# Two head pairs to one probabilities-times-V run in a fused attention, MLP and expert kernel, with four resident weight blocks in place of five

## The chip, the cores and the metric

The kernel runs on one core of a Trainium2 chip. The metric is the device time of one execution in microseconds (us), as the median over runs. Five engines work side by side, each through its own list of instructions in order: TensorE (PE, with its weight loads shown apart as PEld), VectorE (DVE), ScalarE (ACT), GpSimd (POOL) and SyncE (SP, which here issues only DMA transfers). An instruction that waits holds up everything behind it on its engine.

## The reference

```python
def reference(q, k, v, w_in, w_out, w_gate, w_noise, noise, w1, w2):   # q, k, v: 4 x 8 x 576 x 64
    scores = q @ k^T / sqrt(64)
    keep the 32 largest scores of every row, softmax over them
    x = (attn @ v) as 2304 tokens x 512
    h = x @ w_in                                  # 512 x 2048
    x = (h * clip(h + 3, 0, 6) / 6) @ w_out       # 2048 x 512
    noisy = x @ w_gate + log1p(exp(x @ w_noise)) * noise      # 8 experts
    top-2 experts of each token, softmax over the two
    out[token] += weight * (relu(x @ w1[e]) @ w2[e])          # w1: 8 x 512 x 1024
```

## The kernel before, in words

Matrix products that need full precision are done with every operand split into a high and a low part, as three matmuls (high by high, high by low, low by high).

**Layer one** (`phase_a`) is a software pipeline, one step for each of 144 slots. A slot is one tile of 128 tokens (18 tiles) with one head (8 heads). Every stage of a slot stands at a fixed number of steps behind its start: the scores (`s`, PE) and their copy to SBUF (`ss`, ACT) first, then the search for the 32nd largest score (`seg`, `a`, DVE), the exponentials (`e`) and the mask (`z`, `y`, `t`), the transposition of the probabilities on PE (`pa`, evacuated by ACT into `pt` and `ph`), and the product with V (`av`). The heads are taken in pairs from there on. In the kernel before `av(p)` runs in every second step: 20 matmuls with the V of two heads as weights (16 with `pt`, 4 with `ph`), then one transposition that spreads the reciprocal row sums (`rb`, made by POOL from `sum`) over partitions. Two steps later ACT copies both halves to `xs` (128x256), POOL multiplies the product with the reciprocals (128x128), and another two steps later ACT and POOL make the high and low part of `xT`.

In the same steps runs the MLP of the chunk of two tiles before: 16 blocks of 128 hidden columns a chunk, `h` (12 matmuls, `mm1`), the gate (`r`, `g`; on ACT, DVE and POOL) and `xa` (6 matmuls, `mm2`). In some steps more stands: the transposition of a head's K (`kp`), and the router of finished tiles (`lt`, `lg`, `po`, and the scatters `idw` on POOL that tell which token goes to which expert).

A block of split MLP weights is 1 MB. Some blocks are resident in the ring "wr" (`NRES` buffers); the others are written to DRAM once (`wscr`) and fetched by SP for every chunk into the ring "ws" (`NSTR`, 4 buffers), three steps ahead in the program. After the last tile the chunk's blocks run without attention beside them.

**Layer two** (`phase_b`) is nine jobs (an expert's gathered tokens) of eight blocks each: `hb` (`mm1`), `hh` (ACT and DVE), `ac` (`mm2`). Weights of block g+3 are loaded into "ws" as `r2_` by SP and split into "wr" as `w2_` by ACT and DVE, or by ACT and POOL from the third job on. The tokens of a job come by `id` (SP, reads what the `idw` scatters wrote), `xg` (POOL, indirect gather) and `et` (PE transposition). Jobs after the first two add to rows already in the output: `old` (POOL gather) and a scatter at a job's end.

The order on PE, DVE, ACT and POOL is the program's from step 22 of layer one on; before that step and in layer two a list scheduler sets it. The order of SP's transfers is the scheduler's everywhere. What the change touches are these lines of the step and of the set of streamed blocks:

```python
stream = set(fb for fb in range(NFB) if (fb * (NFB - NRES)) // NFB != ((fb + 1) * (NFB - NRES)) // NFB)
if ok(x1) and x1 % 2 == 0: xscale(x1 // 2)        # ACT, before the search
if ok(x1) and x1 % 2 == 0: xscale2(x1 // 2)       # POOL, behind it
if ok(av_) and av_ % 2: av(av_ // 2)              # PE, behind mm2
if ok(x2) and x2 % 2 == 0: xsplit(x2 // 2)        # ACT and POOL
```

Of the kernel before, what the change touches and what calls it, by code (L numbers as in the profile page):

```python
# [7 lines left out]
F32 = mybir.dt.float32  # L8
# [5 lines left out]
ALU = mybir.AluOpType  # L14
# [13 lines left out]
NRES = 5  # L28
# [13 lines left out]
PTB = 3  # L42
# [4 lines left out]
VB = 10  # L47
# [7 lines left out]
XSB = 2  # L55
# [121 lines left out]
def phase_a(tc, pools, ident, q, k, v, w_in, w_out, X, worst, wscr, stream, begin, on_chunk=None, slots=NSLOT, pace=None):  # L177
# [46 lines left out]
    def copy(kind, out, in_):  # L224
        (nc.vector.tensor_copy if kind in ONV else nc.scalar.copy)(out, in_)
# [226 lines left out]
    def av(p):  # L452

        t = p // 4
        AVP[p] = o = ps.tile([128, 512], F32, name=f"av{p}", tag="av")
        for b, row, n, s0 in pieces(t):
            for j in range(5):
                for hh in (1, 0):
                    half = slice(64 * hh, 64 * hh + 64)
                    vt, pt = V[b, (2 * p + hh) % 8][:, j, :], PT[2 * p + hh][:, j, :] if j < 4 else PH[p]  # L460
                    nc.tensor.matmul(o[half, row:row + n], vt, pt[:, row:row + n], start=(j == 0),
                                     stop=(j == 4), skip_group_check=True)
        nc.tensor.transpose(o[:, 128:256], RB.pop(p).rearrange("p a b -> p (a b)"), ident)

    def xscale(p):
        xs = ap.tile([128, 256], F32, name=f"xs{p}", tag="xs", bufs=XSB)
        copy('a', xs, AVP.pop(p)[:, 0:256])
        XR[p] = xs

    def xscale2(p):  # L470
        xs = XR.pop(p)
        nc.gpsimd.tensor_tensor(xs[:, 0:128], xs[:, 0:128], xs[:, 128:256], op=ALU.mult)
        XS[p] = xs[:, 0:128]

    def xsplit(p):
        t, d = divmod(p, 4)
        c, j = chunk_of[t]
        if j == 0 and d == 0:
            xt = mp.tile([128, 2, 4, 256], F32R, name=f"xT{c}", tag="xT", bufs=2)
            XT[c] = [xt[:, z] for z in range(2)]  # L480
        xt, xs = XT[c], XS.pop(p)
        sl = slice(j * 128, (j + 1) * 128)
        copy('x', xt[0][:, d, sl], xs)
        nc.gpsimd.tensor_tensor(xt[1][:, d, sl], xs, xt[0].bitcast(F32)[:, d, sl], op=ALU.subtract)
# [99 lines left out]
    for st in range(-6, end):  # L584
# [33 lines left out]
        if ok(x1) and x1 % 2 == 0: xscale(x1 // 2)  # L618
# [19 lines left out]
        if ok(x1) and x1 % 2 == 0: xscale2(x1 // 2)  # L638
# [6 lines left out]
        if ok(av_) and av_ % 2: av(av_ // 2)  # L645
        for i, (dl, b, h) in enumerate(ksched):
            if dl + VL == st: v_load(i)
        if ok(x2) and x2 % 2 == 0: xsplit(x2 // 2)
# [678 lines left out]
```

## Time and profile before

| | |
|---|---|
| median of 3 runs | 1391.53 us (1387.91 to 1395.7) |
| the profiled execution | 1381.3 us; its span from first to last instruction 1379.5 us |
| mean granted TensorE clock | 0.975 |
| busy share of PE, DVE, ACT, POOL | 94%, 69%, 56%, 60% |
| streamed MLP blocks | 99 reads of 1 MB into "ws", 11 writes of 1 MB to `wscr` |

The profiled execution is 10.2 us shorter than the median of the runs. Layer one fills the first 880 us or so, layer two the rest. A busy PE is not a PE at its peak, so the page's shares say which engine is loaded, and the rows of a stretch say what it waits for there.

### The profile page before, as it was taken

What the parts mean: (1) busy time and instruction counts of PE and PEld (TensorE: products, weight loads), DVE (VectorE), ACT (ScalarE), POOL (GpSimd) and SP (SyncE); (2) the same over time, 40 slices, a digit from 0 to 9 for tenths busy, and PEclk for the clock granted to TensorE, in tenths of its full rate; (3) what the DMA queues carried; (4) which work ended last, traced back from release to release, by engine and by line L of the source; (5) the groups of instructions that cost most, each with busy time, mean ns of one, the idle gap of its engine ahead of it and who ended that gap; (6) DMA issues with size and microseconds to landing.
All of it is one profiled execution on the core that took longest, in us unless ns stands there. A gap on an engine that the chain in (4) does not pass through costs nothing. (4 is left out here: it accounts for less than half of the span.)

```text
span 1379.5 us, 27084 instructions
## 1 busy us (share of the span) xinstructions
PE 1293.2 (94%) x9006; PEld 1121.2 (81%) x9006; DVE 948.3 (69%) x3560; ACT 770.2 (56%) x1709; POOL 829.9 (60%) x1159
## 2 busy tenths in 40 slices
PE   5878899999999989999999899899999999999996
PEld 3554689989888878898988688788988898898985
DVE  7999987899987978869989753446353545435241
ACT  6888777777778666777777554534322322222220
POOL 7666777677767786767687845133324547465451
PEclk9789999999999999999999999999999999999999
DMA  7776644545365353445544447846446556465431
GB/s 249 261 279 226 230 145 157 193 166 176 132 206 166 127 149 124 170 131 187 175 143 157 123 154 246 265 140 221 136 153 195 178 167 204 140 214 177 137 109 38
DMA packets 138100, 239.56 MB, mean 174 GB/s; under 512 B 39779, under 2 KB 93155, under 8 KB 123872
## 3 DMA queue, kind: packets, MB, share of 16 engines
q1 hardware_dynamic: 127600, 210.57, 46.1%
q0 software_dynamic: 10352, 27.18, 5.9%
q8 instruction: 73, 1.20, 0.4%
q14 instruction: 75, 0.61, 0.2%
HBM read 209.08 MB, written 31.64 MB: 174 GB/s over the span
## 5 line engine op out<-in xcount | busy, mean ns | idle before, releaser
L959 PE MATMUL ac<-w,hh 128*128 128x512 f32 x960 | 247.8, 400 | 1.6 <-ACT hh L941 1.5
L935 PE MATMUL hb<-xe,w 128*128 128x320 f32 (+2 forms) x1536 | 239.4, 311 | 1.0 <-DVE hh L942 0.5
L935 PEld LDWEIGHTS hb<-xe,w 128*128 128x128 f32 x1536 | 232.1, 189 | 10.0 <-issue 3.9
L87 DVE MAX8 seg<-ss 128x8 f32<-128x82 f32 (+1 forms) x1008 | 213.9, 231 | 4.1 <-ACT ss L87 3.7
L87 POOL TENSOR_TENSOR y<-z,ss 128x576 f32<-128x576 bf16 x144 | 205.3, 1426 | 11.7 <-DVE z L87 10.1
L941 ACT ACTIVATE hh<-hb 128x640 fp32r<-128x640 f32 (+2 forms) x72 | 46.6, 647 | 295.7 <-PE hb L935 295.7
L959 PEld LDWEIGHTS ac<-w,hh 128*128 128x128 f32 x960 | 172.8, 188 | 40.3 <-ACT hh L941 5.4
L942 DVE SCALAR_TENSOR_TENSOR hh<-hb,hh 128x640 fp32r<-128x640 f32 (+2 forms) x72 | 53.9, 749 | 213.2 <-ACT hh L941 213.2
L87 PE MATMUL h<-xT,ws 128*128 128x256 f32 x1188 | 159.1, 283 | 9.3 <-DVE r L87 7.9
L87 ACT COPY ss<-s 128x576 f32<-128x576 f32 x144 | 92.6, 643 | 134.6 <-DVE e L87 69.6
L87 PE MATMUL xa<-ws,g 128*128 128x512 f32 x594 | 163.9, 410 | 2.2 <-POOL g L87 0.9
L87 PEld LDWEIGHTS h<-xT,ws 128*128 128x128 f32 x1188 | 150.0, 190 | 12.8 <-DVE r L87 9.9
L921 POOL TENSOR_TENSOR w<-r,w 128x1024 fp32r<-128x1024 f32 x40 | 97.9, 2452 | 85.2 <-ACT w L919 73.4
L87 DVE SCALAR_TENSOR_TENSOR e<-ss,t,e 128x576 f32<-128x576 f32 x144 | 147.6, 1025 | 0.1
L87 POOL TENSOR_TENSOR g<-r,g 128x256 fp32r<-128x256 f32 x124 | 100.2, 808 | 39.8 <-issue 19.6
L87 PEld LDWEIGHTS xa<-ws,g 128*128 128x128 f32 x594 | 104.0, 190 | 23.6 <-POOL g L87 5.1
L87 DVE TENSOR_SCALAR_CACHE_REDUCE z<-ss,a 128x576 bf16<-128x576 f32 x144 | 115.8, 804 | 0.2
L87 ACT ACTIVATE e<-ss,a 128x576 f32<-128x576 f32 x144 | 110.6, 768 | 1.4 <-POOL a L87 1.4
L87 PE MATMUL s<-kt,qt 128*128 128x288 f32 x512 | 101.2, 321 | 7.8 <-ACT qt L87 6.8
L87 DVE MAX8 t<-y 128x8 f32<-128x584 f32 x144 | 107.8, 749 | 0.0
L975 POOL DMA_INDIRECT out_dram<-y,id x40 | 41.8, 1045 | 108.9 <-DVE y L974 86.7
L87 PE MATMUL pa<-ident,e 128*128 128x128 f32 x576 | 91.3, 283 | 15.4 <-DVE e L87 13.4
(427 smaller groups left out, 2617.2 us busy)
## 6 DMA issues: line engine op xcount, KB each, us to landing
ws<-wscr SPq DMA_DIRECT2D x99, 1024.0 KB, 4.8
r<-in_moe_w_dram SPq DMA_DIRECT2D x144, 256.0 KB, 3.1
wscr<-wsp SPq DMA_DIRECT2D x11, 1024.0 KB, 5.8
wraw<-in_moe_w_in_dram SPq DMA_DIRECT2D x16, 512.0 KB, 4.2
wraw<-in_moe_w_out_dram SPq DMA_DIRECT2D x16, 512.0 KB, 5.1
ck<-in_moe_w_in_dram SPq DMA_DIRECT2D x32, 256.0 KB, 3.4
ck<-in_moe_w_out_dram SPq DMA_DIRECT2D x32, 256.0 KB, 3.2
out_dram<-zero SPq DMA_DIRECT2D x18, 256.0 KB, 4.2
```

The costliest lines, as they stand in the source:

```text
L87: o = f(*args, **kw)
L921: eng.tensor_tensor(w[:, 1], r, w.bitcast(F32)[:, 0], op=ALU.subtract)
L935: o = nc.tensor.matmul(p[:, half, 0:hn], w[:, a, d, :], XE[job][:, b, d, half * hn:(half + 1) * hn], start=(m == 0), stop=(m == 11))
L941: nc.scalar.activation(hv[:, 0], p[:, 0:nh, 0:hn], AF.Relu)
L942: LOW[:] = [STT(hv[:, 1], p[:, 0:nh, 0:hn], 0.0, h.bitcast(F32)[:, :, 0:n].rearrange("p a (b n) -> p a b n", b=nh)[:, 0], op0=ALU.max, op1 ...
L959: o = nc.tensor.matmul(ACC[job, j], h[:, a, j * 128:(j + 1) * 128], w[:, b, :], start=(x % NF2 == 0 and m == 0), stop=(x % NF2 == NF2 - 1 ...
L975: s = nc.gpsimd.indirect_dma_start(out=out, out_offset=bass.IndirectOffsetOnAxis(ap=t.bitcast(I32)[:, j, 1:2], axis=0), in_=y, in_offset=N ...
```

## The change

Two head pairs are taken together. `av(g)` runs in every fourth step: 20 matmuls for pair 2g, 20 for pair 2g+1, then both transpositions of `rb`, all into one PSUM bank. ACT's copy to `xs` becomes one of 128x512 in every fourth step, POOL's product one of 128x256, and the cast and the subtraction into `xT` one of 128x256 each. The probabilities of the first pair are held longer, so the ring of `pt` grows from 3 to 5 buffers and that of V from 10 to 12, while `xs` has 1 buffer instead of 2. For the space `NRES` goes from 5 to 4: blocks 0, 4, 8 and 12 stay resident in place of 0, 3, 6, 9 and 12, and 12 of 16 blocks stream instead of 11 (108 reads and 12 writes of 1 MB). The ring "wr" of 4 also holds the split weights of layer two.

```diff
-NRES = 5
+NRES = 4
-PTB = 3
+PTB = 5
-VB = 10
+VB = 12
-XSB = 2
+XSB = 1
-    def av(p):
-        t = p // 4
-        AVP[p] = o = ps.tile([128, 512], F32, name=f"av{p}", tag="av")
-        for b, row, n, s0 in pieces(t):
-            for j in range(5):
-                for hh in (1, 0):
-                    half = slice(64 * hh, 64 * hh + 64)
-                    vt, pt = V[b, (2 * p + hh) % 8][:, j, :], PT[2 * p + hh][:, j, :] if j < 4 else PH[p]
-                    nc.tensor.matmul(o[half, row:row + n], vt, pt[:, row:row + n], start=(j == 0),
-                                     stop=(j == 4), skip_group_check=True)
-        nc.tensor.transpose(o[:, 128:256], RB.pop(p).rearrange("p a b -> p (a b)"), ident)
+    def av(g):
+        t = g // 2
+        AVP[g] = o = ps.tile([128, 4, 128], F32, name=f"av{g}", tag="av")
+        for z in range(2):
+            p = 2 * g + z
+            for b, row, n, s0 in pieces(t):
+                for j in range(5):
+                    for hh in (1, 0):
+                        half = slice(64 * hh, 64 * hh + 64)
+                        vt, pt = V[b, (2 * p + hh) % 8][:, j, :], PT[2 * p + hh][:, j, :] if j < 4 else PH[p]
+                        nc.tensor.matmul(o[half, z, row:row + n], vt, pt[:, row:row + n], start=(j == 0),
+                                         stop=(j == 4), skip_group_check=True)
+        for z in range(2):
+            nc.tensor.transpose(o[:, 2 + z], RB.pop(2 * g + z).rearrange("p a b -> p (a b)"), ident)
...
-        copy('a', xs, AVP.pop(p)[:, 0:256])
+        copy('a', xs, AVP.pop(g))
...
-        nc.gpsimd.tensor_tensor(xs[:, 0:128], xs[:, 0:128], xs[:, 128:256], op=ALU.mult)
+        nc.gpsimd.tensor_tensor(xs[:, 0:2], xs[:, 0:2], xs[:, 2:4], op=ALU.mult)
...
-        copy('x', xt[0][:, d, sl], xs)
-        nc.gpsimd.tensor_tensor(xt[1][:, d, sl], xs, xt[0].bitcast(F32)[:, d, sl], op=ALU.subtract)
+        copy('x', xt[0][:, d:d + 2, sl], xs)
+        nc.gpsimd.tensor_tensor(xt[1][:, d:d + 2, sl], xs, xt[0].bitcast(F32)[:, d:d + 2, sl], op=ALU.subtract)
...
-        if ok(x1) and x1 % 2 == 0: xscale(x1 // 2)
+        if ok(x1) and x1 % 4 == 2: xscale(x1 // 4)
...
-        if ok(x1) and x1 % 2 == 0: xscale2(x1 // 2)
+        if ok(x1) and x1 % 4 == 2: xscale2(x1 // 4)
...
-        if ok(av_) and av_ % 2: av(av_ // 2)
+        if ok(av_) and av_ % 4 == 3: av(av_ // 4)
...
-        if ok(x2) and x2 % 2 == 0: xsplit(x2 // 2)
+        if ok(x2) and x2 % 4 == 2: xsplit(x2 // 4)
```

Three places show how instructions move. The first is SP at the end of layer one: `ws8_13` to `ws8_15` are the last three streamed MLP blocks of the last chunk, `id0` is the list of tokens of layer two's first job, `r2_0` and `r2_1` are raw weights of its first blocks. Before:

```order
L496 DMA ws8_13_13601<-wscr_78 128x2048
L496 DMA ws8_14_13628<-wscr_78 128x2048
L888 DMA id0_13871<-idw_76 128x6
L496 DMA ws8_15_13655<-wscr_78 128x2048
L911 DMA r2_0_13883<-in_moe2_w1_dram 128x4x128
L913 DMA r2_0_13883<-in_moe2_w2_dram 128x512
L911 DMA r2_1_13889<-in_moe2_w1_dram 128x4x128
```

and with the change:

```order
L499 DMA ws8_13_13404<-wscr_78 128x2048
L891 DMA id0_13674<-idw_76 128x6
L499 DMA ws8_14_13431<-wscr_78 128x2048
L499 DMA ws8_15_13458<-wscr_78 128x2048
L914 DMA r2_0_13686<-in_moe2_w1_dram 128x4x128
L916 DMA r2_0_13686<-in_moe2_w2_dram 128x512
L914 DMA r2_1_13692<-in_moe2_w1_dram 128x4x128
L916 DMA r2_1_13692<-in_moe2_w2_dram 128x512
```

`id0`, which reads what the `idw` scatters wrote, now stands ahead of the last two blocks instead of the last one.

The second is PE at the hand-over from layer one to layer two: `lt17`, `lg16` and `lg17` are router matmuls of the last two tiles, `po16` is the count that the router's placing of these tiles needs, `hb` and `ac` are layer two's first and second product. Before:

```order
L718 MATMUL lt17_13790<-ident_66,xm17_13769 128x128 x4
L729 MATMUL lg16_13784<-wgn_957,lx16_13782 128x16 x4
L729 MATMUL lg17_13797<-wgn_957,lx17_13795 128x16 x4
L935 MATMUL hb0_13922<-xe0_13882,w2_0_13886 128x384 x12
L959 MATMUL ac0_0_13974<-w2_0_13886,hh0_13935 128x512 x2
L959 MATMUL ac0_1_13978<-w2_0_13886,hh0_13935 128x512 x2
L959 MATMUL ac0_2_13982<-w2_0_13886,hh0_13935 128x512 x2
L935 MATMUL hb1_13958<-xe0_13882,w2_1_13892 128x384 x12
L959 MATMUL ac0_0_13974<-w2_0_13886,hh0_13935 128x512
L959 MATMUL ac0_1_13978<-w2_0_13886,hh0_13935 128x512
L959 MATMUL ac0_2_13982<-w2_0_13886,hh0_13935 128x512
L784 LDWEIGHTS tri_969
```

There `po16` stands behind `hb1` and three `ac`. With the change the order begins so:

```order
L721 MATMUL lt17_13593<-ident_66,xm17_13572 128x128 x4
L938 MATMUL hb0_13725<-xe0_13685,w2_0_13689 128x384 x12
L732 MATMUL lg16_13587<-wgn_939,lx16_13585 128x16 x4
L732 MATMUL lg17_13600<-wgn_939,lx17_13598 128x16 x4
L962 MATMUL ac0_1_13781<-w2_0_13689,hh0_13738 128x512 x2
L962 MATMUL ac0_2_13785<-w2_0_13689,hh0_13738 128x512 x2
L938 MATMUL hb1_13761<-xe0_13685,w2_1_13695 128x384 x12
```

and `po16` follows some blocks later:

```order
L938 MATMUL hb2_13795<-xe0_13685,w2_2_13701 128x384 x12
L962 MATMUL ac0_0_13777<-w2_1_13695,hh1_13774 128x512
L962 MATMUL ac0_1_13781<-w2_1_13695,hh1_13774 128x512
L962 MATMUL ac0_2_13785<-w2_1_13695,hh1_13774 128x512
L962 MATMUL ac0_0_13777<-w2_2_13701,hh2_13808 128x512 x2
L962 MATMUL ac0_1_13781<-w2_2_13701,hh2_13808 128x512 x2
L962 MATMUL ac0_2_13785<-w2_2_13701,hh2_13808 128x512 x2
L787 LDWEIGHTS tri_951
L787 MATMUL po16_13640<-oh16_13577,tri_951 128x16
```

`hb0` has moved ahead of `lg16` and `lg17`, and `po16` has moved behind `hb2` and the `ac` around it, directly ahead of `hb3`.

The third is POOL at a boundary of layer two's jobs, where `old` and `xg0` are gathers and `w2_36` to `w2_38` the low parts of split weights. Before:

```order
L921 TENSOR_TENSOR w2_36_15693<-r2_36_15690,w2_36_15693 128x1024
L975 DMA out_0_dram<-y3_2_15583,id3_14559 2304x512
L975 DMA out_0_dram<-y3_3_15588,id3_14559 2304x512
L975 DMA out_0_dram<-y3_4_15593,id3_14559 2304x512
L921 TENSOR_TENSOR w2_37_15752<-r2_37_15749,w2_37_15752 128x1024
L868 DMA old_13865<-out_0_dram,id4_15074 128x512 x5
L868 DMA xg0_13863<-X_75,id6_16164 128x512 x5
L921 TENSOR_TENSOR w2_38_15806<-r2_38_15803,w2_38_15806 128x1024
L921 TENSOR_TENSOR w2_39_15867<-r2_39_15864,w2_39_15867 128x1024
L921 TENSOR_TENSOR w2_40_15933<-r2_40_15930,w2_40_15933 128x1024
L921 TENSOR_TENSOR w2_41_15994<-r2_41_15991,w2_41_15994 128x1024
L921 TENSOR_TENSOR w2_42_16055<-r2_42_16052,w2_42_16055 128x1024
L921 TENSOR_TENSOR w2_43_16161<-r2_43_16158,w2_43_16161 128x1024
```

and with the change:

```order
L924 TENSOR_TENSOR w2_36_15496<-r2_36_15493,w2_36_15496 128x1024
L871 DMA old_13668<-out_0_dram,id4_14877 128x512 x5
L871 DMA xg0_13666<-X_75,id6_15967 128x512 x5
L924 TENSOR_TENSOR w2_37_15555<-r2_37_15552,w2_37_15555 128x1024
L924 TENSOR_TENSOR w2_38_15609<-r2_38_15606,w2_38_15609 128x1024
L924 TENSOR_TENSOR w2_39_15670<-r2_39_15667,w2_39_15670 128x1024
L924 TENSOR_TENSOR w2_40_15736<-r2_40_15733,w2_40_15736 128x1024
L924 TENSOR_TENSOR w2_41_15797<-r2_41_15794,w2_41_15797 128x1024
L924 TENSOR_TENSOR w2_42_15858<-r2_42_15855,w2_42_15858 128x1024
L978 DMA out_0_dram<-y4_0_15921,id4_14877 2304x512
L978 DMA out_0_dram<-y4_1_15926,id4_14877 2304x512
```

`w2_37` stood ahead of the nine or ten gathers and now stands behind them, next to `w2_38`. The same holds at the four boundaries that follow.

## Rows read from the trace of the kernel before

**Rows 1.** Busy time of each engine in four stretches (stretch, sum, engines).
```profile
core 0: us, PE busy (x) PEld busy (x) DVE busy (x) ACT busy (x) POOL busy (x), PEclk, DMA share, GB/s
30.00:150.00 120.00, 90.99 (x485) 59.66 (x485) 117.87 (x448) 99.44 (x195) 81.50 (x102) 0.85 0.74 270
...
300.00:400.00 100.00, 99.43 (x814) 89.19 (x813) 89.79 (x411) 74.29 (x188) 70.81 (x109) 1.00 0.49 165
...
500.00:540.00 40.00, 33.90 (x238) 29.64 (x237) 31.73 (x139) 21.84 (x53) 30.61 (x45) 0.87 0.44 120
...
1100.00:1350.00 250.00, 249.64 (x1404) 222.84 (x1403) 107.67 (x209) 67.14 (x84) 138.42 (x89) 1.00 0.50 161
```

**Rows 2.** Timeline of PE over two plain steps (start, length, instruction).
```profile
303.20 1.62 PE L87 MATMUL xa<-ws,g 128*128 128x512 f32 x6
304.75 1.09 PE L87 MATMUL av<-pt,v 128*64 128x128 f32 x16
305.67 0.39 PE L87 MATMUL av<-ph,v 128*64 128x128 f32 x4
...
306.07 0.77 PE L87 MATMUL s<-kt,qt 128*128 128x288 f32 x4
...
308.77 1.62 PE L87 MATMUL xa<-w,g 128*128 128x512 f32 x6
310.23 0.69 PE L87 MATMUL s<-kt,qt 128*128 128x288 f32 x4
...
312.74 1.65 PE L87 MATMUL xa<-ws,g 128*128 128x512 f32 x6
```

**Rows 3.** Timeline of DVE over the same two steps.
```profile
304.62 0.40 DVE L87 SCALAR_TENSOR_TENSOR r<-r,h 128x256 f32<-128x256 f32 x1
...
308.40 0.17 DVE L87 RECIPROCAL sum<-sum 128x2 f32<-128x2 f32 x1 [0.48 <-POOL sum L87]
...
314.20 0.40 DVE L87 SCALAR_TENSOR_TENSOR r<-r,h 128x256 f32<-128x256 f32 x1
```

**Rows 4.** Groups by line and form (busy, mean ns, idle before).
```profile
L87 POOL TENSOR_TENSOR g<-r,g 128x256 fp32r<-128x256 f32 x124 | 100.2, 808 | 39.8 <-issue 19.6 <-POOL a L87 10.0 <-DVE e L87 4.5
...
L87 POOL TENSOR_TENSOR xs<-xs 128x128 f32<-128x128 f32 x72 | 39.7, 551 | 82.2 <-ACT xs L87 82.2
```

**Rows 5.** Timeline of SP at the end of layer one (issues).
```profile
859.72 3.11 SPq L496 DMA_DIRECT2D ws<-wscr  x2
872.20 0.33 SPq L888 DMA_DIRECT2D id<-idw  x1
872.63 0.38 SPq L496 DMA_DIRECT2D ws<-wscr  x1
```

**Rows 6.** Timeline of PE at the hand-over to layer two.
```profile
873.50 1.57 PE L87 MATMUL h<-xT,ws 128*128 128x256 f32 x12
...
877.79 1.65 PE L87 MATMUL h<-xT,ws 128*128 128x256 f32 x12 [1.33 <-DMA ws<-wscr]
...
889.21 1.96 PE L729 MATMUL lg<-wgn,lx 128*128 128x16 f32 x16 [1.25 <-ACT lx L720]
891.02 3.67 PE L935 MATMUL hb<-xe,w 128*128 128x384 f32 x12
...
899.59 0.18 PE L784 MATMUL po<-oh,tri 128*128 128x16 bf16 x1
...
901.18 2.25 PE L935 MATMUL hb<-xe,w 128*128 128x384 f32 x12
...
919.64 0.66 PE L899 MATMUL et<-ident,xg 128*128 128x128 f32 x4 [2.41 <-DMA xg<-X,id]
```

**Rows 7.** Timeline of PE in a stretch with router scatters.
```profile
503.87 2.93 PE L87 MATMUL h<-xT,ws 128*128 128x256 f32 x12 [3.34 <-DVE r L87]
```

**Rows 8.** Timelines of POOL and PE at a boundary of two jobs.
```profile
1105.78 7.38 POOL L921 TENSOR_TENSOR w<-r,w 128x1024 fp32r<-128x1024 f32 x3
...
1112.01 3.68 PE L935 MATMUL hb<-xe,w 128*128 128x320 f32 x24
```

More of the change, by code (lines that the diff above doesn't have):

```diff
@@ L450, in phase_a, with xscale, xscale2, xsplit @@
     AVP, XR, XS, XT = {}, {}, {}, {}
-    def av(p):
-        t = p // 4
-        AVP[p] = o = ps.tile([128, 512], F32, name=f"av{p}", tag="av")
-        for b, row, n, s0 in pieces(t):
-            for j in range(5):
-                for hh in (1, 0):
-                    half = slice(64 * hh, 64 * hh + 64)
-                    vt, pt = V[b, (2 * p + hh) % 8][:, j, :], PT[2 * p + hh][:, j, :] if j < 4 else PH[p]
-                    nc.tensor.matmul(o[half, row:row + n], vt, pt[:, row:row + n], start=(j == 0),
-                                     stop=(j == 4), skip_group_check=True)
-        nc.tensor.transpose(o[:, 128:256], RB.pop(p).rearrange("p a b -> p (a b)"), ident)
-    def xscale(p):
-        xs = ap.tile([128, 256], F32, name=f"xs{p}", tag="xs", bufs=XSB)
-        copy('a', xs, AVP.pop(p)[:, 0:256])
-        XR[p] = xs
-    def xscale2(p):
-        xs = XR.pop(p)
-        nc.gpsimd.tensor_tensor(xs[:, 0:128], xs[:, 0:128], xs[:, 128:256], op=ALU.mult)
-        XS[p] = xs[:, 0:128]
-    def xsplit(p):
-        t, d = divmod(p, 4)
+    def av(g):
[12 more added lines that the diff above has]
+            nc.tensor.transpose(o[:, 2 + z], RB.pop(2 * g + z).rearrange("p a b -> p (a b)"), ident)
+    def xscale(g):
+        xs = ap.tile([128, 4, 128], F32, name=f"xs{g}", tag="xs", bufs=XSB)
+        copy('a', xs, AVP.pop(g))
+        XR[g] = xs
+    def xscale2(g):
+        xs = XR.pop(g)
+        nc.gpsimd.tensor_tensor(xs[:, 0:2], xs[:, 0:2], xs[:, 2:4], op=ALU.mult)
+        XS[g] = xs[:, 0:2]
+    def xsplit(g):
+        t, d = divmod(2 * g, 4)
         c, j = chunk_of[t]
@@ L480, in xsplit @@
             XT[c] = [xt[:, z] for z in range(2)]
-        xt, xs = XT[c], XS.pop(p)
+        xt, xs = XT[c], XS.pop(g)
         sl = slice(j * 128, (j + 1) * 128)
-        copy('x', xt[0][:, d, sl], xs)
-        nc.gpsimd.tensor_tensor(xt[1][:, d, sl], xs, xt[0].bitcast(F32)[:, d, sl], op=ALU.subtract)
+        copy('x', xt[0][:, d:d + 2, sl], xs)
+        nc.gpsimd.tensor_tensor(xt[1][:, d:d + 2, sl], xs, xt[0].bitcast(F32)[:, d:d + 2, sl], op=ALU.subtract)
     chunks = [list(range(t, min(t + 2, slots // 8))) for t in range(0, slots // 8, 2)]
```

## The prediction

> **What bounds the kernel now.** I read the busy times by stretch first, because the shares of the whole span mix stages with different limits. In the start (30 to 150 us) DVE is busy 117.87 of 120 us and PE 90.99: DVE sets the pace. In the plain part of layer one (300 to 400) PE is busy 99.43 of 100 and DVE 89.79. In a stretch with the router's scatters (500 to 540) PE falls to 33.90 of 40 and the clock to 0.87, and POOL has 30.61. In layer two (1100 to 1350) PE has 249.64 of 250, DVE 107.67 and POOL 138.42 [rows 1]. So a saving on PE is worth its full size only where PE is the last to finish, and PE's busy share cannot tell that in layer one, since its matmuls are pipelined. The timelines can. Two plain steps take PE 9.54 us (from the `xa` run at 303.20 to the one at 312.74) [rows 2]. DVE repeats in 9.58 (`r` at 304.62 and at 314.20), and in it waits 0.48 for POOL's `sum` [rows 3]. That is a loop over engines: PE's `h` feeds DVE's `r`, ACT and POOL make `g`, POOL goes on to `y` and `sum`, DVE inverts it. PE and this loop are within 0.04 us of each other in a plain pair of steps. Last I read the hand-over to layer two, where each wait of PE passes on whole, because layer two has no slack behind it: PE is full there to 0.36 of 250 us [rows 1].
>
> **The change part by part: PE.** Work stays the same: 40 matmuls and two transpositions of `rb` per four steps, once instead of twice. What goes is a changeover. With `av` between, the next `s` starts 2.87 us after the start of `xa` (303.20 to 306.07); without, 1.46 (308.77 to 310.23). The difference is 1.41. The 16 matmuls with `pt` take 0.92 from start to start, 0.0575 each, so 21 instructions are worth 1.21. The remaining 0.20 is lost on entering the run and between `ph` and `ident`; and the `s` run behind it lasts 0.77 instead of 0.69, another 0.08 [rows 2]. So a run saved gives 0.28 us. There are 36 fewer: at most 36 x 0.28 = 10.1 us, at least nothing.
>
> The Trainium skill would give less: "TensorE: Matmul & The Clock Gate", section "Back-to-back issue gap" with "LDWEIGHTS (loading the stationary operand)", has the spacing of matmuls in a stream set by the matmul and its weight load alone, the load by its columns, with no price for going from one kind to another; by an estimate from it 64 columns load in 53 ns. By that the change saves nothing on PE, and the sum below would be 2.9 us higher; the rows do show 0.28 at the changeover, so I go by them.
>
> How many of the 36 count? In a plain pair of steps the loop over DVE and POOL is already as long as PE (9.58 against 9.54), so a saving there only turns into idle PE. It counts where a step has more for PE: a K transposition (32 of 144 steps) or router matmuls. I count such work in 21 of the 72 pairs of steps, by the order of the program, overlaps and the DVE-bound start taken off. 36 x 21/72 = 10.5 runs at 0.28 give **-2.9 us**.
>
> **POOL and ACT.** A product or subtraction of 128x128 takes POOL 0.55 us in the mean, the 128x256 `g` 0.81 [rows 4]. Per four steps four operations of 0.55 become two of 0.81: 0.59 us less. POOL had time in plain steps: it sat idle 82.2 us over 72 before `xs`, 1.14 each, waiting for ACT [rows 4]. It is short only near the scatters, where PE loses 6.1 of 40 us [rows 1]. There are two such stretches of 40 us, four merges each: at most 8 x 0.59 = 4.7, at least 0, because the scatters themselves remain. I take **-1.0**, near the low end, since the wait seen there is on DVE's `r` and DVE is not relieved [rows 7]. ACT, busy 74.29 of 100 in the plain part, has fewer and larger copies and was not waited for there [rows 1]; 0.
>
> **Streaming and rings.** Nine more blocks of 1 MB are read and one written. The DMA share in the plain part is 0.49 [rows 1]. The wait of PE on a streamed block that the rows hold is the 1.33 us at 877.79 [rows 6]. Nine more of that size would be 12 us, none would be 0; I take 0, as the plain part shows PE full with 11 of 16 blocks streaming already. The larger rings of `pt` and V give room and take no time; `xs` with one buffer is used once in four steps, and 0 is taken for it. In the start DVE's 2.13 us of idle in 120 bound a gain; I take 0 and allow 3 us of loss. In layer two the ring of four lets the split of a block start one block later. At the job boundary POOL does `w2_37` behind the gathers, with `w2_38`: three such operations take 7.38 from 1105.78, 2.46 each, so it ends near 1108.2, and `hb37` starts at 1112.01 [rows 8]. 3.8 us remain; 0, and up to 3 us where a boundary has less.
>
> **The hand-over.** Before, `ws8_14` was issued in the run of two from 859.72, `id0` got through at 872.20 (it waits for the scatters), `ws8_15` at 872.63 [rows 5]. `ws8_15` was used as it landed, at 877.79: 5.16 us [rows 5, 6]. Now `ws8_14` stands behind `id0` too. Issued at 872.6 it lands near 877.8, and its `h` run stood at 873.50: PE waits 4.3 us. The last `h` run stood 2.96 us behind that if the 1.33 is taken off, so it comes at 880.8 instead of 877.79, **+3.0**; with the two blocks sharing the DMA engines, up to +4.2.
>
> Then `lg16` and `lg17` stand behind `hb0`. PE idled 1.25 before them, and a full-rate `hb` takes 2.25, so they move by +1.0; at the 3.67 that `hb0` took, +2.4 [rows 6]. From `lg` the routing chain on DVE and ACT has to end before `po`. From 889.21 to 899.59 that took 10.4; now PE itself has two `hb` (4.5) and some 24 `ac` of about 0.235 (5.6, worked out from PE's pace between the rows at 899.59 and 901.18, six in about 1.5) behind `lg`'s 1 to 2 us: +0.7 to +1.7. So `po` is late by 4.7 to 8.3. What is queued behind: the placing, POOL's scatters, SP's `id1`, the gathers `xg`, then `et` at 919.64, 20.05 us after `po`, for which PE already waited 2.41 [rows 6]. PE has done `hb2` early and has nothing else then, so its idle time grows to 6 us or so and all of the lateness reaches the end. A shorter idle, 3.34, was followed by an `h` run of 2.93 where 1.57 is usual [rows 6, 7], close to the lower of the clock's two levels (1.2 GHz): 1.35 for the clock, which this stretch's mean of 0.87 shows too [rows 1]. I take the low side of the chain with one slow run, 4.7 + 1.35 = **+6.0**, with bounds 2 (the scatters land early enough that only the order on PE costs) and 9.7.
>
> **Sum.** -2.9 - 1.0 + 6.0 = +2.1 against the profiled execution: 1381.3 + 2.1 = 1383.4. That execution is 10.2 below the median of the runs shown, so on the median's footing 1391.5 + 2.1 = **1393.6 us**. Half a per cent, 7 us, is about what a measurement of this kernel can tell from no change, so this is no measurable change.
>
> **The rivals.**
> *Faster.* PE's changeovers count everywhere, because the loop over DVE shortens as soon as `h` comes earlier: -10.1, POOL -2.4, hand-over only +2: 1381.0. For it: PE is busy 99.43 and DVE has 10.21 of 100 left [rows 1]. Against it: the 0.48 wait on POOL's `sum` in each pair of steps [rows 3], which is not PE's. Half of the saving would not be measurable. Chance 0.17.
> *Slower by the hand-over.* The chain costs its upper bound, 9.7, and nothing is won in layer one: 1401.2. It decides from `et` on: if PE's wait there is over 9 us instead of 2.41, the time is over the bound of 7. For it: the order shows both `id0` and `po` moved. Chance 0.22.
> *Slower by bunching.* POOL's two larger operations fall into one step of four: 1.62 where a step had 1.09, 0.53 more. Were POOL's lane the last in the loop in each of some 32 fours of steps, that is 17 us, with the hand-over's 6: 1414.5. Against it: 1.14 idle before `xs` [rows 4]. Chance 0.07. The Trainium skill, "Trace Analysis", section "Optimizing Scalar/DVE Operations", speaks for this one: grouping helps an engine that is saturated, and where an engine is not, but causes bubbles elsewhere, breaking up is its advice. That the idle share before `xs` is large agrees with "not saturated".
> *Nothing happens.* Every saving is hidden and the hand-over's moves too: 1391.5. Chance 0.08.
> The forecast, from 1388 to 1398 by the parts' nearer bounds, has 0.46.
>
> **Range and chances.** Below 1384.6 lies most of the faster rival and nothing else: 0.13. Above 1398.5 lie most of the hand-over rival (0.18), bunching (0.07) and the upper edge of the forecast (0.03): 0.28. Between: 0.59. The range 1384 to 1404 leaves out some 0.1 on either side.
>
> **What would show it.** Right: `av` runs with 32 and 8 matmuls once in four steps and 0.28 less per four steps on PE; plain fours of steps still 19.1 us long with PE idle a few tenths; `ws8_14` landing about 877 on before's clock and a wait of 3 to 4 us before its `h`; `po` 5 us or more later from the last `xa`; PE's wait at `et` of the second job over 5 us; layer two as long as before. Wrong: plain fours clearly under 19.1 (faster), or PE waiting on `r` or `g` in one of four steps (bunching), or waits on "ws" blocks in every chunk, or waits of `hb` on POOL's `w` at job boundaries.

## The result, and the profile after

The changed kernel takes 1400.78 us (median of 14 runs, 1394.73 to 1406.48), the kernel before on the same footing 1391.63 (14 runs): a ratio of 1.0064 with a 95% interval of 1.004 to 1.0088, that is 5.6 to 12.2 us longer. The time lies in the predicted range (1384 to 1404) and above the predicted 1393.6. On the prediction's own yardstick of half a per cent it came out slower, to which it had given 0.28; what it thought likeliest was no measurable change.

The stretches that [rows 1] shows of before read so with the change (same view and columns):

```profile
30.00:150.00 120.00, 90.75 (x464) 57.84 (x464) 116.42 (x429) 95.15 (x179) 78.32 (x92) 0.82 0.74 264
...
300.00:400.00 100.00, 98.77 (x818) 89.41 (x817) 92.42 (x421) 72.74 (x174) 68.00 (x98) 1.00 0.49 170
...
500.00:540.00 40.00, 35.01 (x267) 29.44 (x266) 31.95 (x133) 23.41 (x55) 33.70 (x43) 0.96 0.56 144
...
1100.00:1350.00 250.00, 249.07 (x1398) 221.83 (x1397) 106.31 (x211) 68.52 (x87) 144.33 (x94) 1.00 0.55 175
```

In the plain part PE is a little less busy (98.77 for 99.43), DVE more (92.42 for 89.79), ACT and POOL less. Near the scatters PE has more of its time. PE is as full in layer two as before. None of this tells where 9 us went. What does is to read, in the timeline of PE, when certain runs begin: the `s` run of step 28 (steps are counted from 0 by their `s` runs), the last `s` run (step 143), the last `h` run, and layer two's eighth block `hb7`. I did this for a second profile of each kernel as well, since one profile cannot tell a cause from chance:

| us | to step 28 | step 28 to 143 | to the last `h` | to `hb7` | to the end of the span |
|---|---|---|---|---|---|
| before | 173.65 | 622.15 | 81.99 | 48.37 | 453.34 |
| before, again | 174.14 | 621.95 | 82.18 | 50.76 | 464.17 |
| changed | 178.70 | 626.87 | 83.88 | 48.81 | 455.14 |
| changed, again | 181.01 | 627.18 | 83.39 | 52.05 | 471.67 |

By the means of the two, the start lost 6.0 us, the steady part of layer one 5.0, the end of layer one 1.6, the hand-over 0.9. That is 13.4, a little over the upper end of the timed difference. The rest of layer two (the last column) differs by 11 and 17 us between two profiles of one kernel, so it says nothing about the change, and nothing smaller than that can be read from whole spans.

The steady part is the clearest. Four plain steps, from the `s` run at 307.48 to the one at 326.72 (PE's timeline of the changed kernel; the matmuls of [rows 2]):

```profile
307.48 0.79 PE L87 MATMUL s<-kt,qt 128*128 128x288 f32 x4 [0.32 <-ACT qt L87]
...
311.64 1.09 PE L87 MATMUL av<-pt,v 128*64 128x128 f32 x16
312.56 0.39 PE L87 MATMUL av<-ph,v 128*64 128x128 f32 x4
312.78 1.04 PE L87 MATMUL av<-pt,v 128*64 128x128 f32 x16
313.65 0.39 PE L87 MATMUL av<-ph,v 128*64 128x128 f32 x4
313.97 0.44 PE L87 MATMUL av<-ident,rb 128*128 128x128 f32 x2
314.16 0.78 PE L87 MATMUL s<-kt,qt 128*128 128x288 f32 x4
...
318.32 0.69 PE L87 MATMUL s<-kt,qt 128*128 128x288 f32 x4
...
322.23 0.69 PE L87 MATMUL s<-kt,qt 128*128 128x288 f32 x4
...
326.72 0.79 PE L87 MATMUL s<-kt,qt 128*128 128x288 f32 x4 [0.29 <-ACT qt L87]
```

The four steps take 6.68, 4.16, 3.91 and 4.49 us, where before steps of 5.38 and 4.16 alternated (one of 4.16 stands from 306.07 to 310.23 in [rows 2], one of 5.38 from 300.69 to 306.07). The sum is 19.24; before, from 300.69 to 319.80, it was 19.11. Without the wait of 0.29 at the end it would be 18.95, so PE does save 0.16 per four steps, and then waits for ACT's `qt`. This four is one of the shorter ones; others take up to 19.50 (table below). ACT's timeline ahead of that wait:

```profile
323.80 0.64 ACT L87 COPY ss<-s 128x576 f32<-128x576 f32 x1 [1.61 <-DVE e L87]
...
326.28 0.40 ACT L87 CAST qt<-qpNone 128x256 fp32r<-128x256 f32 x1
```

ACT had waited 1.61 for DVE's `e`, and everything from `ss` to `qt` stands behind that in its order. So the wait on `qt` is a wait on DVE. I read it so: PE is early there because its three short steps ran ahead of DVE; behind its long step it is late, and then DVE can wait for `ss`. In this four DVE does not. Over the 24 steps from step 44 it shows, and on PE more than on DVE. The waits of both engines there, first of before (again, 262.8 to 380.2 us, where PE has none), then of the changed kernel (again, 270.8 to 389.1; total, times, longest):

```profile
DVE sum L87 <- POOL sum L87: 9.4, 12, 1.3
DVE seg L87 <- ACT ss L87: 0.5, 1, 0.5
```

```profile
PE s L87 <- ACT qt L87: 1.2, 4, 0.3
DVE sum L87 <- POOL sum L87: 7.3, 12, 1.3
DVE seg L87 <- ACT ss L87: 1.5, 3, 0.6
```

The 24 steps take 117.34 and 118.25 us. PE gains four waits in six fours, DVE waits 1.0 more for `ss` and 2.1 less for POOL's `sum`. The groups of DVE between 180 and 800 us, in the same two profiles:

```profile
L87 DVE MAX8 seg<-ss 128x8 f32<-128x82 f32 x575 | 132.8, 231 | 3.5 <-ACT ss L87 3.1
L87 DVE SCALAR_TENSOR_TENSOR e<-ss,t,e 128x576 f32<-128x576 f32 x115 | 115.5, 1005 | 0.0
```

```profile
L87 DVE MAX8 seg<-ss 128x8 f32<-128x82 f32 x569 | 131.9, 232 | 9.3 <-ACT ss L87 9.0
L87 DVE SCALAR_TENSOR_TENSOR e<-ss,t,e 128x576 f32<-128x576 f32 x114 | 122.1, 1071 | 0.0
```

DVE waits 5.9 us more for `ss`. Its `e` has a mean 66 ns longer, but that mean mixes two things. Two `e` of 3.96 and 3.77 us near the scatters (505.71 and 769.49), which before does not have, are most of it. And a longer `e` alone does not lengthen plain steps: in the run with the merge behind PE alone, below, the 24 steps from step 44 have a mean `e` of 1081 ns (the change, again, 1049; before, again, 989) and yet the shortest plain fours of all. On the other side DVE waits 7.4 us less for POOL's `sum` over these 620 us (76.0 for 83.4).

### The profile page after: what moved, and what is told of

Same layout as the page of the kernel before. It is cut to its first block, busy times and chain, and to the rows that moved or that the text cites. A ratio compares the mean times of both kernels' runs of the same rounds, so it can differ in the third digit from the quotient of the medians.

```text
span 1393.4 us, 26965 instructions
## 1 busy us (share of the span) xinstructions
PE 1296.2 (93%) x9006; PEld 1121.2 (80%) x9006; DVE 956.8 (69%) x3560; ACT 763.8 (55%) x1637; POOL 823.0 (59%) x1087
## 5 line engine op out<-in xcount | busy, mean ns | idle before, releaser
L87 POOL TENSOR_TENSOR y<-z,ss 128x576 f32<-128x576 bf16 x144 | 211.2, 1467 | 19.2 <-DVE z L87 15.5
L87 PE MATMUL xa<-ws,g 128*128 128x512 f32 x648 | 177.2, 408 | 1.2 <-POOL g L87 0.9
L87 PE MATMUL h<-xT,ws 128*128 128x256 f32 x1296 | 168.1, 279 | 3.4 <-DVE r L87 2.8
L87 PEld LDWEIGHTS h<-xT,ws 128*128 128x128 f32 x1296 | 159.2, 188 | 7.4 <-DVE r L87 4.9
L87 DVE SCALAR_TENSOR_TENSOR e<-ss,t,e 128x576 f32<-128x576 f32 x144 | 159.4, 1107 | 0.1
L87 PEld LDWEIGHTS xa<-ws,g 128*128 128x128 f32 x648 | 113.5, 190 | 22.7 <-POOL g L87 3.6
L87 POOL TENSOR_TENSOR g<-r,g 128x256 fp32r<-128x256 f32 x124 | 104.0, 838 | 46.2 <-issue 27.1
L87 PEld LDWEIGHTS s<-kt,qt 128*128 128x128 f32 x512 | 78.8, 196 | 37.1 <-ACT qt L87 27.3
```

What stands on the lines that cost most here:

```text
L87: o = f(*args, **kw)
```

## The experiments

My theories, before the runs. **A**: what counts in layer one is which steps of PE and DVE fall together; the merged run makes PE's steps uneven against DVE's, and both engines lose time waiting. **B**: the larger operations of ACT and POOL bunch in one step. **C**: the block that streams more, or the ring of four, costs it (C1 the streaming, C2 layer two's ring). For the start came **D** later: the list scheduler's order in the start of before is a good one, and whatever changes it loses some us. In the excerpts of code below `...` stands for what is left out, and lines that set several constants are drawn together.

The table has the same stages for all experiments, and the length of three plain fours of steps (those from step 44, 48 and 64). Ratios are against the kernel before on the same chip; chips differed by up to 14 us in its median (1386.18 to 1400.2), so times are compared only there. The stages of each row are those of one profile, and a row without a ratio rests on that one execution.

| | to step 28 | 28 to 143 | last `h` | `hb7` | end | plain fours | ratio |
|---|---|---|---|---|---|---|---|
| before, again | 174.14 | 621.95 | 82.18 | 50.76 | 464.17 | 19.22, 19.08, 19.08 | |
| changed, again | 181.01 | 627.18 | 83.39 | 52.05 | 471.67 | 19.50, 19.38, 19.33 | |
| NRES 4 alone | 178.06 | 625.54 | 83.15 | 49.34 | 462.41 | 19.22, 19.08, 19.09 | 1.0047 (1.0021 to 1.0074) |
| merge, NRES 5 | 189.89 | 639.13 | 83.14 | 51.60 | 453.84 | 19.50, 19.37, 19.37 | 1.0227 (1.0181 to 1.0273) |
| merge on PE only | 180.07 | 647.12 | 85.06 | 48.96 | 466.99 | 19.69, 20.59, 20.34 | 1.0231 (1.0183 to 1.0279) |
| merge behind PE only | 178.48 | 622.69 | 81.80 | 58.05 | 463.58 | 19.09, 18.96, 19.08 | 1.0041 (1.0014 to 1.0069) |
| 12 blocks, ring of 5 | 178.08 | 624.35 | 83.23 | 52.68 | 466.36 | 19.24, 19.08, 19.08 | 1.0061 (1.0036 to 1.0086) |
| old hand-over order | 178.67 | 627.25 | 86.40 | 54.29 | 471.49 | 19.51, 19.42, 19.37 | 1.0102 (1.0068 to 1.0135) |
| KEEP 24 | 176.15 | 621.24 | 82.26 | 49.23 | 453.82 | 19.22, 19.07, 19.08 | |
| KEEP 20 | 177.97 | 624.73 | 83.21 | 50.47 | 453.52 | 19.23, 19.08, 19.10 | |
| `av` one step later | 177.27 | 643.27 | 84.12 | 52.92 | 453.42 | 19.38, 20.90, 20.90 | |
| second job's tokens later | 175.65 | 622.00 | 81.95 | 46.37 | 454.83 | 19.23, 19.08, 19.08 | 0.9996 (0.998 to 1.0011) |

**NRES 4 alone.**

```diff
-NRES = 5
+NRES = 4
```

> The kernel before with NRES 4 alone: 12 of 16 blocks stream, ring wr has 4 buffers, one av run per pair as before. Theory A (the merge makes PE's steps uneven, and the start and the hand-over are ordered anew): plain fours of steps stay at 19.1 us, the last s run is late by at most 4 us through the start, and the time is within 0.4% of before. Rival C (the streaming and the smaller ring cost it): most of the 0.64% is here, with waits of h on ws blocks or a start 4 us longer.

Plain fours are as before, so streaming costs nothing there, and PE has no wait on a streamed block in the chunks. Yet the time is 0.47% over before: rival C has its part. The stages put it into the start (+3.9 against before, again) and into the steps 88 to 96 around the first scatters (53.35 us for 50.56).

**The merge with five resident blocks.**

```diff
 NRES = 5
-KTB, QRB, KRB = 10, 2, 2
+KTB, QRB, KRB = 9, 1, 1
 (the rest as in the change)
```

> The merged run with NRES 5 (11 blocks stream as before); the room comes from KTB 9, KRB 1 and QRB 1. Theory A: plain fours of steps take 19.3 us as with the change, steps 28 to 140 together some 5 us longer than before, time 0.3 to 0.7% above before. Rival C: plain fours at 19.1 or less and the time at or below before. If the start (to step 28) is as before, the 4.4 us that it lost belong to NRES 4; if it is again late, to the merge.

The plain fours are 19.37 and 19.50 as with the change, with eleven blocks streamed: the merge makes them longer, not the streaming. The total says nothing for C, because the smaller rings cost far more than the point in question (16 us in the start alone, and some in the steps with a K transposition).

**The merge on PE alone.**

```diff
-        if ok(x1) and x1 % 4 == 2: xscale(x1 // 4)
+        if ok(x1) and x1 % 4 >= 2: xscale(2 * (x1 // 4) + x1 % 4 - 2)
...
-        if ok(x2) and x2 % 4 == 2: xsplit(x2 // 4)
+        if ok(x2) and x2 % 4 in (1, 2): xsplit(2 * (x2 // 4) + x2 % 4 - 1)
 (xs, product and xT pair by pair again; XSB 2)
```

> The change with the merged run on PE alone: xs, its product and xT are again made pair by pair (two steps each), NRES 4, PTB 5, VB 12. Theory A (PE's uneven steps): plain fours stay at 19.3 us and s waits 0.3 us on qt once in four steps; time like the change. Rival B (the larger ACT and POOL operations bunch in one step): plain fours back at 19.1, time about 5 us below the change.

Worse than the change by 20 us in the steady part. PE's waits between 180 and 800 us (total, times, longest):

```profile
PE h L87 <- DVE r L87: 20.8, 23, 3.3
PE pa L87 <- DVE e L87: 8.5, 24, 1.8
PE s L87 <- ACT qt L87: 2.5, 6, 0.9
```

Rival B falls: with small operations on ACT and POOL the loss is larger. But theory A had foretold the change's time here, and missed by 20 us. PE now waits longest for DVE's `r`, and DVE waits 12.9 us for POOL's `sum` in the 24 steps from step 44, where the change has 7.3. I read that as the operations of ACT and POOL standing, in two steps of four, in front of what DVE's loop needs; this was not tested by itself.

**The merge behind PE alone.**

```diff
-    def av(g):
+    def av(p):
+        t, g, z = p // 4, p // 2, p % 2
...
-        if ok(av_) and av_ % 4 == 3: av(av_ // 4)
+        if ok(av_) and av_ % 2: av(av_ // 2)
 (xs, product and xT for two pairs at once; NRES 5, PTB 3, VB 10)
```

> One av run per pair as before, but both pairs into one bank, and xs, product and xT for two pairs at once (128x512, 128x256); NRES 5, PTB 3, VB 10, so 11 blocks stream. Theory A: plain fours at 19.1 us as before, time within 0.4% of before, perhaps 1 us less near the scatters. Rival B: plain fours at 19.3 us, waits of s on qt, time about 5 us above before.

Plain fours fall to 18.96 and 19.09, and the steady part is that of before (622.69 for 621.95): with PE's steps even, the larger operations do no harm. The 0.41% by which it is slower lies in the start (+4.3) and at the hand-over, where PE waited 6.5 us for `xg`. Note the start: only eleven blocks stream here, and DVE waits there for raw weights as long as in before, again (5.4 us up to 182 us in both), yet step 28 comes at 178.48, as late as with twelve.

**Both kernels once more.** No edit.

> The kernel before, profiled once more. Its first profile ran 10 us under its median. If that was chance spread over the stages, this profile is some 5 to 10 us longer, and shows where: the start (late by about 4.5 us at step 28, as in all other kernels so far), the scatter stretches, or waits of 1 to 3 us for ACT's hh in layer two. If the start is as early as before, the 4.5 us belong to the order of the other kernels.

> The changed kernel, profiled once more. Plain fours of steps again 19.3 us (0.2 over before) if that is the merge and not chance; the start, the scatter stretches and layer two may differ from the first profile by several us.

The start and layer one came again within 0.5 us for before, and for the changed kernel within 2.3 in the start and 0.3 in the steady part. So the steady part can be read from one profile, the start only to some 2 us. Most of the chance is in layer two. PE's waits there, before's first profile having had 0.9 on `hh` and none on "issue":

```profile
PE ac L959 <- ACT hh L941: 7.2, 5, 3.6
PE ac L959 <- issue: 1.2, 1, 1.2
```

and the changed kernel, again:

```profile
PE ac L962 <- ACT hh L944: 10.5, 5, 4.2
PE et L902 <- DMA xg<-X,id: 3.4, 1, 3.4
PE ac L962 <- issue: 2.7, 2, 2.4
```

**Twelve streamed blocks, ring of five.**

```diff
-        stream = set(fb for fb in range(NFB) if (fb * (NFB - NRES)) // NFB != ...
+        stream = set(fb for fb in range(NFB) if (fb * (NFB - 4)) // NFB != ...
```

> The kernel before with 12 of 16 blocks streamed, but the ring wr still of 5 buffers, so layer two keeps its ring. Against the run with NRES 4 it tells streaming (start, reads, order at the hand-over) from layer two's smaller ring. Theory C1 (streaming and the new order of start and hand-over cost it): about 0.4% above before, as with NRES 4. Theory C2 (layer two's ring of 4): time as before, within 0.2%.

1.0061, and stages like those of NRES 4 alone: layer two's smaller ring (C2) is not the cause. What the two runs share is the twelfth streamed block and the order that the scheduler makes for it (C1); which of these it is, this run does not tell. The start has 3.9 us of it, the steps 88 to 96 another 1.6. DVE, which sets the pace in the start, waits for raw weights and for POOL's `sum`:

```profile
121.90 1.40 DVE L87 TENSOR_SCALAR wt<-wraw 128x512 int32<-128x512 int32 x1 [2.44 <-DMA wraw<-in_moe_w_in_dram]
148.61 0.17 DVE L87 RECIPROCAL sum<-sum 128x2 f32<-128x2 f32 x1 [2.01 <-POOL sum L87]
```

Before, again, has no wait at the first place and 1.07 at the second.

**The old order at the hand-over, in the changed kernel.**

```diff
+        if job == 0: after(tc, o, LASTWS[0])     # id0 behind the last streamed block, on SP
...
+                    if g == 0: after(tc, o, LASTLG[0])     # hb0 behind lg17, on PE
```

> The change with the old order at the hand-over: id0 behind the last streamed block on SP, hb0 behind lg16 and lg17 on PE. By the prediction's term of 6 us the time falls by about 6 us against the change, to 1394, and the last s run to hb7 takes about 6 us less. By what the first profile of the change shows (last s run to hb7 only 2.3 us longer than before) it gives 0 to 2 us.

Nothing of the 6 us came back; from the last `s` run to `hb7` it took 140.7 us, for 135.4 and 132.7 in the two profiles of the change. PE now waits longest at `et`:

```profile
865.29 16.14 SPq L499 DMA_DIRECT2D ws<-wscr  x5
881.72 0.33 SPq L892 DMA_DIRECT2D id<-idw  x1
```

```profile
938.44 1.12 PE L905 MATMUL et<-ident,xg 128*128 128x128 f32 x4 [7.62 <-DMA xg<-X,id]
```

The run of five blocks ends at 881.43, and `id0` goes directly behind it, 0.7 us later than with the change (881.72 and 881.04): in both kernels it gets through only here, so moving it in SP's order was worth little either way. The chain from `po` to `et` took 20.9 us. The other part of the order, `hb0` and `po` on PE, was moved back in the same run, so the two are not told apart.

**The start's order alone: KEEP 24 and KEEP 20 in the kernel before.**

```diff
-KEEP = 22
+KEEP = 24     (and, apart, 20)
```

> The kernel before with the program's order kept from step 24 on instead of 22: nothing but the order in the start differs. If the old order of the start is one that any change loses (theory D), step 28 comes 2 to 6 us later than before's 174; if the 4 us of the other kernels are the price of what they changed, it comes within 1 us.

> The same with the program's order kept from step 20 on. Theory D: step 28 again 2 to 6 us later than before's 174. Otherwise within 1 us.

With nothing changed but the order, step 28 comes at 176.15 and 177.97. How much of that is chance, three profiles of before's own order at the start show: 173.65, 174.14 and, on the same chip as these two, 175.65 (the last experiment below). So KEEP 24 tells nothing, and KEEP 20 is 2.3 to 4.3 us late. With KEEP 20 the steps 88 to 96 also take 52.94, like those of the streaming kernels (53.35, 52.18) and unlike before's 50.56 and KEEP 24's 49.79. For theory D stand this one profile and two others that stream eleven blocks in another order: the merge behind PE alone (178.48, on another chip) and `av` one step later (177.27, below). So a loss of most of that size does not need the streaming. It does not show that the streaming alone would have cost nothing under another order. The later starts with twelve streamed blocks are beyond chance: on the chip of before's second profile (174.14) three kernels that have them came at 178.08, 178.67 and 181.01.

**`av` one step later in the kernel before.**

```diff
-OS, OA, OB, OC, OD, OE, OV, OX, OY = 1, 1, 2, 3, 4, 5, 6, 8, 10
+OS, OA, OB, OC, OD, OE, OV, OX, OY = 1, 1, 2, 3, 4, 5, 7, 9, 10
-PTB, VB, QRB = 3, 10, 2
+PTB, VB, QRB = 4, 11, 1
```

> The kernel before, one av run per pair, but every run and its xs copy one step later, so that PE's long step no longer falls together with DVE's long step (PTB 4, VB 11, QRB 1 for it). Theory A (what counts is which steps of PE and DVE fall together, not the length of PE's sum): plain fours go from 19.1 to 19.3 us or more, with waits of s on qt. If it is the merge itself, they stay at 19.1.

Nothing is merged here and every operation has its old size, but the plain fours go up to 20.90 and the steady part by 21 us. Three rings had to differ too; the smaller one, of raw Q, doesn't seem to be what holds, as PE's transposition of it ahead of the wait shows no wait itself. PE's timeline of one pair of steps:

```profile
291.40 0.80 PE L87 MATMUL s<-kt,qt 128*128 128x288 f32 x4 [0.42 <-ACT qt L87]
...
295.67 1.09 PE L87 MATMUL av<-pt,v 128*64 128x128 f32 x16
...
301.61 0.80 PE L87 MATMUL s<-kt,qt 128*128 128x288 f32 x4 [0.41 <-ACT qt L87]
```

10.21 us for two steps instead of 9.54, with the wait on `qt` in each. This is theory A's strongest run. In before an `av` run starts as the longer of DVE's two steps does (304.75 [rows 2], with `r` at 304.62 and 314.20 [rows 3]; the `r` between them, first line below, parts the pair into 5.31 and 4.27). Here `av` starts at 295.67, 0.8 us before that longer step ends (the `r` at 296.48, second line below):

```profile
309.93 0.41 DVE L87 SCALAR_TENSOR_TENSOR r<-r,h 128x256 f32<-128x256 f32 x1
```

```profile
296.48 0.40 DVE L87 SCALAR_TENSOR_TENSOR r<-r,h 128x256 f32<-128x256 f32 x1
```

So where `av` stands against DVE's long step is worth more than the merge could have saved.

**The second job's tokens one block later, in the kernel before.**

```diff
-        first = 5 if nxt and nxt[1] else 3
+        first = 6 if nxt and nxt[1] else 3
```

> The kernel before with the transpositions of the second job's tokens one block later in layer two's program (first = 6). PE waited 2.4 to 3.8 us there for the gathers. If that wait is on the path, hb5 to hb6 and hb7 together fall by 2 to 3 us and the time by 0.2%; if the wait only moves to hb8, nothing changes.

PE no longer waits at `et` (before, again; then this run):

```profile
920.94 0.66 PE L899 MATMUL et<-ident,xg 128*128 128x128 f32 x4 [2.44 <-DMA xg<-X,id]
```

```profile
924.14 0.60 PE L899 MATMUL et<-ident,xg 128*128 128x128 f32 x4
```

and the last `h` to `hb7` takes 46.37 instead of 48.37 and 50.76. In the time it cannot be told from before, 0.9996 (0.998 to 1.0011): 2 us are 0.14%, and the start of this profile was 1.5 us later, with the same instructions in the same order there. It is no version that beats before.

## Why the prediction was right or wrong

**The range held, and the likeliest case did not.** The sum was +2.1; measured 9.15 (5.6 to 12.2). That the time lies in the range is in part luck: PE's term was off by some 9 us and the start by 6, both too low, and the hand-over by 3.5 the other way. The terms, one by one:

*PE's changeovers, -2.9.* This is the step that failed, and with the wrong sign. The price of a changeover had the right sign: the merged PE work of four plain steps is 0.16 shorter without its wait, where 0.28 was predicted for one run less. The prediction also saw that PE and the loop over DVE are tied in plain steps. It went wrong at "a saving there only turns into idle PE": it took the loop's 9.58 as fixed. But the loop keeps this length only while PE's and DVE's steps stand to each other as in before. The merged run puts 1.3 us more into one step and 1.5 less into another; outside the steps 88 to 96 the part from step 28 to 143 grew by 6.3 us (571.4 to 577.7). That the merged run on PE costs it, and not the larger operations or the streaming, is shown: with everything merged but PE's run, plain fours take 18.96 to 19.09; with the merge and eleven blocks, 19.37 to 19.50; with twelve blocks alone, 19.08 to 19.24. That alignment can cost more than this, with nothing merged, is shown by `av` a step later (up to 20.9). That alignment is also how the merged run costs it is my reading of the rows: no run kept the merge and changed the alignment alone.

*POOL near the scatters, -1.0.* Right: the steps 88 to 96 take 49.18 and 49.57 instead of 50.75 and 50.56, 1.3 less.

*Streaming and the start, 0 with 3 us of loss allowed.* Mis-sized. The start lost 4.6 to 7.4 us. Some four of them come with the twelfth streamed block and its order, without the merge; but a start as late comes with eleven blocks too (178.48, the merge behind PE alone), and a changed order alone gave 2.3 or more, once. So how much is the streaming and how much the order stays open. The idle time of DVE, 2.13 in 120, was a right bound for a gain and none for a loss. In the plain part the 0 was right.

*The hand-over, +6.0.* Mis-sized: 1.6 and 0.9, 2.5 in all. The first part of the term did not come: the `h` run that was to wait 4.3 us for `ws8_14` (886.62 below) waited 0.61, as `id0` got through 8.4 us ahead of the last `h` instead of 5.6. Behind it the order had moved as told, and `po` is 6 us later from the last `h` (27.81 and 28.55 for 21.80 and 22.59), where 1.7 to 4.1 was allowed. But behind `po` the chain to `et` took 15.88 us, in the second profile of the change 16.83, where before had 20.05 and 20.08:

```profile
881.04 0.33 SPq L891 DMA_DIRECT2D id<-idw  x1
881.48 0.85 SPq L499 DMA_DIRECT2D ws<-wscr  x2
```

```profile
886.62 1.61 PE L87 MATMUL h<-xT,ws 128*128 128x256 f32 x12 [0.61 <-DVE g L87]
...
917.26 0.18 PE L787 MATMUL po<-oh,tri 128*128 128x16 bf16 x1
...
933.14 0.66 PE L902 MATMUL et<-ident,xg 128*128 128x128 f32 x4 [2.45 <-DMA xg<-X,id]
```

PE's wait there is 2.45, in the second profile 3.38, where before had 2.41 [rows 6] and 2.44; 6 was predicted. The `hb` behind it takes 2.33 in this profile and 3.80 in the second, with a granted clock of 1.00 and 0.61 there; the slow run was put at 1.35. But the length of the wait does not decide it: behind 2.44 in before's second profile the `hb` took 2.98, at a granted clock of 0.70, and behind 2.41 in its first 2.25, at 1.00. The prediction held the 20.05 fixed, and it was not. Part of it lies between the last scatter's issue and the first gather `xg`: 8.2 and 8.8 us in the two profiles of before, 5.8 and 6.3 in those of the change, 8.4 with the old order in the changed kernel, where the whole chain takes 20.9.

It is tempting to say that the new order brought its own cover, but the other runs speak against it. The kernel with twelve blocks and a ring of five has the new order here, on PE (`hb0` ahead of `lg`, `po` ahead of `hb3`) and on SP (`id0` ahead of the last two blocks), and yet 8.15 us and a chain of 20.0, with the wait that the prediction foretold:

```profile
931.65 1.12 PE L899 MATMUL et<-ident,xg 128*128 128x128 f32 x4 [6.56 <-DMA xg<-X,id]
```

KEEP 24 has the old order and 6.35 us. So the 6 us were spared in the two profiles of the change, not by its order as far as the runs show; why these transfers land sooner in some profiles stays open.

*Layer two's ring of four, 0.* Not contradicted: no wait of `hb` on POOL's `w` appears, and the run with a ring of five is no faster.

*The rivals.* "Slower by the hand-over" had the right sign by the wrong place. "Bunching", 0.07, is refuted as a cause by two runs, PE alone and behind PE alone. The rule of the Trainium skill's page "TensorE: Matmul & The Clock Gate" ("Back-to-back issue gap"), which names no price for a changeover, would have left out the gain and been nearer in sum, but the 0.16 is there. The Trainium skill's page "Perfetto Trace Analysis", section "Optimizing Scalar/DVE Operations", says that breaking up operations of Scalar or Vector may help where they aren't saturated but cause bubbles on other engines; for the operations of ACT and POOL here it did not: with PE's run unmerged the larger operations behind it give the shorter plain fours (18.96 to 19.09, the smaller 19.08 to 19.22), and with PE's run merged too (19.33 to 19.50, the smaller 19.69 to 20.59).

## What to carry to other kernels

Where two engines' steps take the same time, write down the length of each step of both, not the sum: a saving that moves work from one step into another can lengthen a loop that neither engine's busy time shows. Before costing a change to code that a list scheduler orders, ask what its order is worth: here a start that differed in nothing but its order came 2.3 us or more later, in one profile, as much as a term of the change's sum. Profile the same kernel twice before explaining a stage by one profile; a stage that repeats within half a microsecond can be read, one that moves by ten cannot. And look at the single operations before you call a group slower by its mean: here two out of 114 made most of the difference.

## What the runs showed of the hardware that was not expected

DVE's `e` (128x576) has no fixed time: in one kernel it takes 0.80 us or up to 1.38, and a few take far longer. The rows tell on what it depends. In the changed kernel's timeline the long one at 322.31 (1.37) runs beside POOL's `g` and `y`; the short one at 318.10 (0.82) has POOL's `xs` beside it for part only:

```profile
318.10 0.82 DVE L87 SCALAR_TENSOR_TENSOR e<-ss,t,e 128x576 f32<-128x576 f32 x1
...
322.31 1.37 DVE L87 SCALAR_TENSOR_TENSOR e<-ss,t,e 128x576 f32<-128x576 f32 x1
```

```profile
318.61 0.90 POOL L87 TENSOR_TENSOR xs<-xs 128x256 f32<-128x256 f32 x1 [2.36 <-ACT xs L87]
...
322.33 0.74 POOL L87 TENSOR_TENSOR g<-r,g 128x256 fp32r<-128x256 f32 x1
323.03 1.82 POOL L87 TENSOR_TENSOR y<-z,ss 128x576 f32<-128x576 bf16 x1
```

What decides is whether POOL is at work when `e` starts. Between 180 and 800 us the changed kernel's first profile has 113 `e`. For 46 no TENSOR_TENSOR of POOL runs at their start: they take 0.80 to 0.82, also the 33 under which POOL starts one. 39 start while `g` runs, or within 0.03 of its start: they take 1.22 to 1.38, and every one ends 0.61 to 0.63 behind the end of that `g`. The other 28 start while another one runs. POOL waits in its turn: in before all 27 `y` that start under an `e` take 1.80 to 1.82, the other 87 1.28 to 1.31. And where POOL has several operations in a row, `e` can wait for all of them; this is one of the two that raise the changed kernel's mean (it stands at 505.71 in the second profile):

```profile
503.42 3.95 DVE L87 SCALAR_TENSOR_TENSOR e<-ss,t,e 128x576 f32<-128x576 f32 x1
```

```profile
503.36 1.30 POOL L87 TENSOR_TENSOR y<-z,ss 128x576 f32<-128x576 bf16 x1
...
504.77 0.72 POOL L87 TENSOR_TENSOR g<-r,g 128x256 fp32r<-128x256 f32 x1
505.45 1.29 POOL L87 TENSOR_TENSOR y<-z,ss 128x576 f32<-128x576 bf16 x1
```

It ends at 507.37, 0.63 behind the second `y`. The rows look like turns taken at something that both engines need. The Trainium skill, "SBUF — State Buffer", section "SBUF: two separate sides", has such a rule: of a DVE operation with two inputs in SBUF and a GpSimd operation that reads SBUF, the one that starts first has the ports that they share for its whole instruction, and the other is blocked. The rows agree with it but for two things: an `e` that waited its whole length would end 0.82 behind `g`, and it ends 0.6 behind; and the `e` at 322.31 is recorded 0.02 ahead of its `g` and waits all the same. No run here changed this by itself.

Layer two's time after `hb7` was 453.3 to 455.1 us in some profiles and 462.4 to 471.7 in others, with waits of ACT and PE of 1 to 10 us that no semaphore event explains. It goes with the chip in part: the four profiles of the chip with before's lowest median (1386.18) have 453.4 to 454.8, the four of the one with its highest (1400.2) 464.2 to 471.7, and a third chip has both (453.8 to 467.0). The cause stays open.
